# S4 convolution with a SwiGLU gate on one core: mirrored token tiles, 32x32 tiles in the tokens' second transform stage, and halved first and last steps

## The chip, the cores and the metric

The kernel runs on one core of one Trainium2 chip. The metric is device microseconds of one execution, as the median of several runs. TensorE is called PE below, its weight loads PEld; VectorE is DVE, ScalarE is ACT, GpSimd is POOL, and SyncE, which issues most DMAs, is SP.

## What is computed

`u` holds 2048 tokens of 512 channels. The tokens are normalised, and the result goes two ways: through a long convolution along time, whose kernel of 2048 taps is generated from 128 complex modes a channel, and through a feed-forward network with 1792 hidden channels. The output is the input plus the convolution times the gate. Cut to what matters (`A`, `Bc`, `Cc` and `dt` come from the other inputs):

```python
xn = _layernorm(u)
P = exp((dt * A)[:, :, None] * l)                       # 512 x 128 x 2048
K = einsum("dn,dnl,dn->dl", Cc, P, dt * Bc).real
y = irfft(rfft(pad(xn^T)) * rfft(pad(K)))[:, :2048]     # length 4096, per channel
s = y^T + xn * Dskip
h = (silu(xn @ w_gate) * (xn @ w_up)) @ w_down
out = u + s * silu(h)
```

## The kernel before, in words

**Stages.** The convolution is done by transforms as matmuls. Time t is written as 32 * t1 + t2, with 64 values of t1 and 32 of t2. A token tile `j` of 16 holds 128 rows: two values of t2 by the 64 values of t1; before, they are the neighbours t2 = 2j and 2j + 1. Stage 1 of the tokens (L549) transforms over t1 with fp16 halves, six matmuls of 512 columns a tile; ACT copies both results (L553), and they go to DRAM as `ax_d` (L554). The taps of the convolution are generated channel by channel (POOL L1061 and L1069, ACT L1084 to L1086, DVE L1104 and L1110, PE L1136), transformed over t1 (L1169) and written to `ak_d`.

Stage 2 goes over eight groups `n` of frequencies by two halves `c` of the channels, 16 blocks in all. Each block loads 512 KB of `ak_d` and 512 KB of `ax_d` into the buffers `ak` and `ax`, and the matrices `gj` of its group once. A block of the taps (L1222, called a k block below) and a block of the tokens (L1229, an x block) have each 16 fp32 matmuls of 256 columns, on tiles of the PE array of 64 rows by 32 columns, eight side by side, so in two rounds. A matmul in fp32 shows as two records in the trace. ACT copies the taps' result out of PSUM (L1239); DVE multiplies it with the tokens' in four instructions (L1247, L1249) and POOL combines these (L1251, L1252). After two blocks an inverse over frequencies follows (L1269, 32 matmuls on tiles of 32 by 32, 16 side by side, so also two rounds), whose result ACT and DVE take out (L1277, L1279) and SP writes to `bs_d` (L1281). After the eighth group of a channel half, the final step can begin (L1316): SP loads `bs_d` (L450, 512 KB), the input again (L1301) and the gate, four matmuls give the convolution of two token tiles and a channel half, DVE multiplies by the gate (L1335), POOL adds the input (L1338) and SP and ACT issue the output (L1342). The last two token tiles, 14 and 15, are done one by one over all channels (L1316, L1323, L1324, L1326).

The network runs beside this in units: 24 matmuls of 256 columns give a gate or an up projection of 256 tokens by 256 hidden channels (L685), ACT and DVE apply silu and the product (L706, L708) and split it into fp16 halves (L710 and L711), and six matmuls of 512 columns a token tile add it to the down projection (L727). L736 is the silu of its result. The weights are loaded in 512 KB pieces, their sum of squares taken on ACT (L590), a power of two as scale made of it on DVE (L621 to L625), and they are split into a high fp16 half on ACT (L655) and a low one on DVE (L656).

**Start.** SP loads the token tiles, `idh` (an identity for transposes) and the weights. DVE takes mean and variance (L485, L486) and an inverse root by three steps of Newton for two tiles at once (L491 to L499, eleven instructions), ACT and DVE make the fp16 halves (L511 to L513), PE transposes them (L522) and DVE copies them out (L528).

**Order.** A planner simulates tasks with given durations. The order of the tasks is a string, `LIST`, two characters a task; the places of the buffers in one SBUF arena are another, `PLACES`. The planner then only assigns eight PSUM banks and fills gaps of PE before the first units with warm-up matmuls (L1425). Each engine works through its own part in order. A DMA waits in its issuing queue until the eighth one before it in that queue has landed.

Of the kernel before, what the change touches and what calls it, by code (L numbers as in the profile page):

```python
# [9 lines left out]
F32 = mybir.dt.float32  # L10
# [9 lines left out]
P = 128  # L20
# [17 lines left out]
SWITCH = 0.095  # L38
TRANSPOSED, TR_US = 4, 1.7
# [11 lines left out]
    "(h(k%B(m$f(d$c$d)1%4$g)2$k$l$n%6%A%C(l(n(w&L&M(x%D)U$h$i$j)3%E)$$o)]$m$t%<%=%>)^%G&U&V&W(q(o(p(J(K)F):%F$u%H%I$p"
    "%?$q$r%L%M&i)G)%)&&`$s%@&a%J&X);)<$v(r%K-<&c&d&e&N)=)>&j%N%O(i)'&f&O).)/)0(^-=)?&P-A-B-C(j&Q&R->&Y&l&g&o&p&]&^(N"
    "(O(P(Q-?(y(z&m&n&S&T(s(t&Z&[)_-@-D-M({-F)H(u(v)`(|-Q)g-K)h-H-Z-E-J-R-O-G)I)P-L-N-U-X-I)Q#I)R-Y#F-[(}-S-T)i-n-w)j"
    "-]-a-e-j-b-W-P-V-^-l)@-o-g.+.,.--p-q-s)S-h-i-k.*)4)T-c-d)A)#-u-v-x)B-r)()C)D-_-t.../-f.0)5)*-m-y-z)))+),.1)E-`-{"
    "-|.8.9.3.4.2.;)V)W.:.>.6.<.5.7.G.B%P)X)Y.E.F.?.@.D.M.[.A.C.H)a)-)c.I.Z.N)b)6)7)d-}.&.=.J#H)8)9.%.$.#.'.).r.b.c%W"
    "%X)J%i%j.O%k)L.P)k)l)s)t.v.()K)M.w.x)Z.K.R)[.L*%.d.e.T.U*&*'.W)N)O)u._*.*/.V.].X.f.Q.s.t.u.S&b.Y.a.^.`%n.g)e)f%R"
    ")v)}.y.h.i%l.j.m&k.k%Q%V%`%o%p)m%m)o%q.l)n)p*#*$*6/,*7.n.o)q%T*:*<.{.|%U.q%a%d/'.p%e*8*9.z.}%S*;*=%r&)%f%b%c)r*("
    "**/$/#/%/)/&/()w)y/+/2/3///1/5&'/4/6/-/.)x/0/*/:/</A/7*>)z){*?*0*2/G*)*+)|/8/9/B*@%Y*A*1/>/;/@*,*-%Z/=/?/D/N*3%]"
    "/H/`%[%^%s%_/a*H*[/P/R*c/I%t/b%u/_/c/C/E/K&s/O/J/L%v/M&w/Q*B*D/d*4*5/F*C*E%w/S*F&x*I*J*L&v&t&u&z/e/t*K&q&{/T&r&|"
    "&y'#&}','-%x*d*G'$/U/g*M*N/V'%/Y'./W'/'>'?/f/Z'&*k*l*s0K'5'6*O*t*u*v/X/[''/]'0'@'B/j'3'C/m'E'F/o/n/^'1*P%y*Q*X'D"  # L60
    "*Y%z&#'7'2%{*e'*'+/h/i%g&$&%&&'(/s04*f/q%h/p*]/z&(%|%}&**^0(*Z/w0'/u050L/k'4/v/l*_*`*R*T/y/{/}/|/r0#/x0$*S00*U0="
    "'90?06070P0Q0R*V*W*g*a*b0M0N*}0O090S+#0+0-08':*w';'<020;0T0U0V'K+$0)0*0:0,*h0.')0<0/0103*x0W0>0@'='80%0&0e0X0s0Y"
    "0[0^0_0a+%0`0A0B*m*n0b0Z0]*o*p0d*i*j0C0G'J0t*y0F+&0D'I*q0E+*'A0h'P'^0H0m*r++1&0f*z*{*|0k0l+'0g0i+(+)+,1%1<+.0J0I"
    "0|0n0j0c+-1=1>1?0o0p0z+=+D+E1@1#0u+/0{0v0}0q0r1A1,+L1-0x+M#G1/1'0w0y1('G+0+1+21)1++31B1C1.101L1E1F'H'O'T+:'L'M1*"
    "1G1a'Q1J'N'R+;'g1D1$1112+<'S1K131H'p'q1Q1N+4'r+5'h'i1P'U+T141518+U't'_16'`+V'V171T191;'w+W1m1I+6+71R1S1U1M'u1n1V"
    "1W+>1X1:1t+X1Y1['v'x1v+?1`1Z1x2*1u1w+Y+@+A1O1]'X2)+8+9'j's1^'[']'k'l1_'m'Y'b+Z'n+[1q'c2+2,'Z'd1o1i1k'e'f1s2-2.2/"
    "+F+H'W+]1p1r1g1h1j+G+I1d1f+N1b1c1e20+J+K21+P22231l'a1y+^2=252429+B+C+O+Q'o2F2726282:1z+_+`1{+a2D2E2;2>2Y2[2]2?2@"
    "2G+b+g2Z2L+R2A2H2U2B+c2<2M2r2C2I2N+S2c+h+i2_2e3k5-2O2Q2W+d2q2u2P2R2S2T+o2V2s+k2t3^2^2`2a2b2d2J2K2v2w+j+l+e+f1|2$"
    "2#3m3`1}2%2&2x+m+n2X2f2g3n3o3a2h3l3_3q3p3t2y3d4S3u3s2(+p3r3w3c3b3g3h3v3f2'2i2k+y2|2j5+4_,%2l2m3e2n3#3$3%3',&,'3&"
    "2o3(2z2{2}+w,(3i2p3j3x4'4(3)3*3.,-,.3y3z3+4{4$3931,53|334%3}494)32354&3,3-,)7K30344#3=3{+q3/+x3B3:3D3F3;3<3@,*3A"  # L70
    "3C4Q4*36374a+s3>3?3H,++r,,+t3G3I3K3M3N483O3P3J3Q+u3L,6,7+z+{+|+},#38+v3E3R3S3T,$70474:4<4;4=4?5,4A5l4T4V4R4>4@4C"
    "3U4,3Y3X3V4U,8,93W3Z4B4W4b4d4-4/4[4X4.7J5.505/4Y4Z4^4]4+40437/4`4e424144463]3[454c4g4f4h4i4j4k4z,/,0,17f,2,34y51"
    "557g5452534D4K4E,:575Q5R5w4F4G4H564N4O4P4|4}4I4J,45$4L,>,?5#5(5'4l4m5%5&4M4v5k6Z4s,;4n4o5)4w4x4p4q,F5*,@,A4r585x"
    "4t4u,<,=595B,G,H5C5D5?5@5<5=,I5S5T5y5:5;5A5V5m5U5W5X5>5Z5Y,B5{,C5z5|6%5o6$6#5[5]5}6[6'8(5n6]656_5p5q,X5s6&5F,J5r"
    "665t,K6`6^6a6b,D,E,L,M5u67686h,`,a6A5v6(6,,h6c,i,p6)6d6f626-6*6e6:6/6960636=6;6<6>6?5E5G5I5H5J5M5N6@,N,O,V6g6i81"
    "6j5K6.6k6+645L5P6l6n6m6o6B6F6p,W6C7.6D615O6q6r6E6J7^7L6G6H,q7[,r,P7@5^,Q6I6K,R5b775c6L7R5e5h5i6s6z5f,S7I,b6{5d,Y"
    "6t6w6x7%6y6}7#,c7$6u6v5_5`715a6M6N7M7N7O,Z7;7)7]7C7(6W7B6X6Y6Q6R6O6P897273747&6S7*7:7D5g7E7A6T6U7_7a6V6|7F76,[7'"
    "78,],^,d,e,_7x,s,t7`7<5j8A7y8B,j887Q,l7P877S79,T,U,y7+,k,m8I7w8.,u,v,z,{,f,g8/8@7=-&7e,n,},o-'8J8%7p7z8:8<7b7c7U"
# [1394 lines left out]
```

## Time and profile before

| | |
|---|---|
| median of three runs | 581.22 us (581.16 to 582.86) |
| the profiled execution | 585.73 us, of which its span in the trace 583.8 us |
| granted clock of PE, mean | 0.997 |
| busy: PE, PEld | 570.9 us (98%), 409.1 us (70%) |
| busy: DVE, ACT, POOL | 422.5 us (72%), 342.6 us (59%), 325.8 us (56%) |
| moved by DMA | 93.62 MB; from HBM 56.40 MB read, 32.90 MB written |

A row of the slices gives the busy share of an engine in tenths for 40 equal slices of the span, 14.6 us each. A row of the groups gives engine, operation, output and input, the number of records, then busy time and mean ns of one, then idle time before. A row of the timeline or of the chain gives the start in us, the length in us, the engine and the line; `x24` at its end counts the records in it, and a bracket gives the idle time before and what ended it. "ACTq" and "SPq" are the queues' own time of issuing DMAs.

### The profile page before, as it was taken

The page shows a single profiled execution, that of the slowest core. Times are in us where ns is not written, and L with a number is a line of the kernel's source. Part 1 is how long each engine was busy: PE and PEld are TensorE (multiplying, and loading weights), DVE is VectorE, ACT ScalarE, POOL GpSimd, SP SyncE. Part 2 cuts the span into 40 slices and gives each one's busy share as a digit, 9 for nine tenths or more (in the row PEclk, how much of TensorE's full clock was granted, in tenths as well). Part 3 has the DMA queues.
Part 4 walks back from the last instruction along what each step waited for, and adds up shares of the span by engine and source line. Part 5 has one row for each costly group of instructions (what it writes and reads, how often), then busy time and mean ns, then how long its engine had stood idle before and what let it go on. Part 6 is the DMA issues. An engine that isn't in the chain of part 4 may idle for free.

```text
span 583.8 us, 18173 instructions
## 1 busy us (share of the span) xinstructions
PE 570.9 (98%) x7523; PEld 409.1 (70%) x7523; DVE 422.5 (72%) x980; ACT 342.6 (59%) x699; POOL 325.8 (56%) x301
## 2 busy tenths in 40 slices
PE   8999999999999999999999999999999999999976
PEld 3788885476885687848776688766866665678732
DVE  6878889537689787985889969877768585653342
ACT  5997677658565367777867889847652423321011
POOL 0154522479986369649799699879135155312140
PEclk9999999999999999999999999999999999999989
DMA  7886542341006150256622086378798878889986
GB/s 245 241 292 199 165 154 72 56 172 43 10 4 125 38 137 2 73 121 206 120 57 69 25 218 123 116 196 231 253 226 246 283 231 258 220 263 260 248 239 176
DMA packets 112434, 93.62 MB, mean 160 GB/s; under 512 B 51104, under 2 KB 96928, under 8 KB 112352
## 3 DMA queue, kind: packets, MB, share of 16 engines
q1 hardware_dynamic: 109856, 90.10, 55.4%
q10 hardware_dynamic: 2496, 2.36, 1.4%
q8 instruction: 59, 0.97, 0.7%
q14 instruction: 23, 0.19, 0.1%
HBM read 56.40 MB, written 32.90 MB: 153 GB/s over the span
## 4 chain that ended last, share of the span: by engine, by line
PE 93%; DMA 3%; ACT 1%; issue 1%; SPq 1%; DVE 0%; ACTq 0%; DVEq 0%
PE p L685 50%; PE p L727 25%; PE p L1136 5%; PE p L1222 3%; PE p L1229 3%; PE p L1316 2%; PE p L1269 2%; DMA arena<-bs_d 2%; PE p L549 2%; PE p L1169 2%; DMA wd<-in_B_w_gate_dram 1%; SPq L471 1%; PE p L785 1%; ACT wg L590 0%; ACTq L1342 0%
## 5 line engine op out<-in xcount | busy, mean ns | idle before, releaser
L685 PE MATMUL p<-arena,wg 128*128 128x256 f16 x1344 | 154.6, 273 | 0.5 <-ACT arena L553 0.5
L685 PE MATMUL p<-arena,wu 128*128 128x256 f16 x1344 | 154.9, 273 | 0.0
L727 PE MATMUL p<-wd,arena 128*128 128x512 f16 x672 | 152.5, 380 | 0.0
L685 PEld LDWEIGHTS <-wg 128*128 128x128 f16 x1344 | 130.2, 98 | 21.6 <-issue 2.8
L685 PEld LDWEIGHTS <-wu 128*128 128x128 f16 x1344 | 130.4, 98 | 20.3 <-issue 2.9
L727 PEld LDWEIGHTS <-arena 128*128 128x128 f16 x672 | 64.0, 98 | 76.0 <-issue 6.1
L1069 POOL TENSOR_TENSOR arena<-arena 128x1536 f32<-128x1536 f32 x32 | 90.8, 2842 | 24.5 <-PE p L1136 7.5
L708 DVE SCALAR_TENSOR_TENSOR p<-p,shc,arena 128x512 f32<-128x512 f32 x56 | 42.1, 755 | 49.7 <-PE p L685 35.1
L1061 POOL TENSOR_TENSOR arena<-arena 128x1024 int32<-128x1024 int32 x32 | 62.4, 1955 | 15.6 <-DVE arena L821 5.4
L710 ACT CAST arena<-p 128x512 f16<-128x512 f32 x56 | 32.4, 587 | 65.8 <-DVE p L708 38.7
L706 ACT ACTIVATE arena<-p,inv 128x512 f32<-128x512 f32 x56 | 38.6, 689 | 54.7 <-PE p L685 43.0
L711 DVE TENSOR_TENSOR arena<-p,arena 128x512 f16<-128x512 f32 x56 | 37.9, 683 | 19.2 <-ACT arena L710 16.1
L1104 DVE TENSOR_TENSOR arena<-arena,p 128x512 f32<-128x512 f32 x64 | 43.6, 681 | 7.2 <-ACT p L1085 4.4
L1338 POOL TENSOR_TENSOR arena<-arena 128x512 f32<-128x512 f32 x12 | 15.1, 1267 | 56.5 <-DVE arena L1335 22.9
L1085 ACT ACTIVATE p<-p,halfpi 128x512 f32<-128x512 f32 x64 | 41.8, 660 | 1.4
L1086 ACT ACTIVATE p<-arena 128x512 f32<-128x512 int32 x64 | 37.6, 602 | 7.5 <-PE p L1169 3.7
L1084 ACT ACTIVATE p<-arena 128x512 f32<-128x512 int32 x64 | 38.5, 605 | 5.3 <-DVE arena L711 3.1
L1251 POOL TENSOR_TENSOR arena<-arena 128x512 f32<-128x512 f32 x16 | 20.3, 1274 | 28.6 <-DVE arena L1247 13.6
L1252 POOL TENSOR_TENSOR arena<-arena 128x512 f32<-128x512 f32 x16 | 20.4, 1275 | 26.0 <-PE p L1169 13.1
L1136 PEld LDWEIGHTS p<-arena 128*32 128x32 f32 x2048 | 29.4, 110 | 4.8 <-issue 2.7
L1110 DVE SCALAR_TENSOR_TENSOR arena<-arena,p 128x256 f32<-128x256 f32 x64 | 26.4, 413 | 8.6 <-ACT p L1086 5.1
L1136 PE MATMUL p<-arena 128*32 128x64 f32 x2048 | 32.2, 220 | 0.0
(182 smaller groups left out, 792.4 us busy)
## 6 DMA issues: line engine op xcount, KB each, us to landing
ax_d<-arena SPq DMA_DIRECT2D x32, 256.0 KB, 3.0
ak_d<-arena SPq DMA_DIRECT2D x16, 512.0 KB, 5.9
arena<-ak_d SPq DMA_DIRECT2D x16, 512.0 KB, 4.6
arena<-ax_d SPq DMA_DIRECT2D x16, 512.0 KB, 5.2
bs_d<-arena SPq DMA_DIRECT2D x32, 256.0 KB, 4.1
arena<-in_A_u_dram SPq DMA_DIRECT2D x62, 128.0 KB, 3.7
arena<-in_B_w_down_dram SPq DMA_DIRECT2D x14, 512.0 KB, 5.3
arena<-bs_d SPq DMA_DIRECT2D x14, 512.0 KB, 8.2
```

The lines of the kernel that those rows point to most:

```text
L685: T.matmul(pg.t[:, i * 256:(i + 1) * 256].rearrange("p (a t) -> p a t", a=2), w[:, wl, d, i * P:(i + 1) * P], x[:, :, xl, d, :], start=(k ...
L706: add("ACT", 0.69, lambda: S.activation(sg.f32(), pg.t, AF.Silu, scale=inv[:, c, 0:1]), rd=[pg], wr=[sg], c=1, pr=e)
L708: add("DVE", 0.75, lambda: V.scalar_tensor_tensor(pu.t, pu.t, shc[:, c:c + 1], sg.f32(), op0=ALU.mult, op1=ALU.mult), rd=[sg], wr=[pu], c= ...
L711: add("DVE", 0.7, lambda: V.tensor_tensor(hh.view(F16)[:, 512:1024], pu.t, hh.view(F16)[:, 0:512], op=ALU.subtract), rd=[pu], wr=[hh], c=1 ...
L727: T.matmul(z.t, h[:, hl, i * 256 + t * P:i * 256 + (t + 1) * P], w[:, wl, i], start=(c == 0 and i == 0 and k == 0), stop=(c == NC - 1 and ...
L1061: G.tensor_tensor(a, h_[:, :, :, None].to_broadcast([P, 2 * GT, 4, 8]), l_[:, :, None, :].to_broadcast([P, 2 * GT, 4, 8]), op=ALU.add)
L1069: G.tensor_tensor(e, p_[:, :, :, None].to_broadcast([P, 3 * GT, 4, 8]), q_[:, :, None, :].to_broadcast([P, 3 * GT, 4, 8]), op=ALU.mult)
L1084: add("ACT", 0.62, lambda: S.activation(tc_.t, a(), AF.Abs, scale=SIN_SCALE), rd=[an], wr=[tc_], pr=pr)
L1085: add("ACT", 0.7, lambda: S.activation(tc_.t, tc_.t, AF.Sin, bias=halfpi, scale=-1.0), rd=[key("ones")], wr=[tc_], c=4, pr=pr)
L1086: add("ACT", 0.62, lambda: S.activation(ts.t, a(), AF.Sin, scale=SIN_SCALE), rd=[an], wr=[ts], pr=pr + 0.2)
L1104: V.tensor_tensor(o[:, :, 0:64].rearrange("p d (s j) -> p d s j", s=2), e[:, :, 0:64].rearrange("p d (s j) -> p d s j", s=2), t[:, :, None ...
L1136: T.matmul(kt[h * 32:(h + 1) * 32, (r * GD + dd) // 4], o[:, ri, dd + h, 64:96], o[:, ri, dd + h, 0:64], start=(ri == 0), stop=(ri == 1), ...
```

## The change

Token tile `j` now holds t2 = 16 + j and its mirror 16 - j (tile 0: 16 and 0), so that stage 2 of the tokens can work on sums and differences of the two. In stage 1 ACT copies one of the two results and DVE makes the sum and the difference (two new instructions for each of 15 tiles; ACT has one copy less there, tile 0 keeps both). The sums and differences are stored in `ax_d` as separate groups, 32 rows each. An x block has still 16 fp32 matmuls, now on tiles of 32 by 32, so in one round; its results lie in four PSUM banks, 256 columns each, instead of two full ones. k blocks and inverses are as they were. `gj` shrinks from 320 to 256 KB a group, `bs_d` gets an order of rows in which every final step reads contiguous pieces of 4 KB.

In the first steps, the first gate weight is loaded ahead of token tiles 2 and 3, in the place of `idh`, which moves to ACT's queue; an ACT table is loaded early; tiles 0 and 1 are normalised one by one, with two steps of Newton (7 instructions for one tile, 9 for two); the first gate weight is split in halves, so that the first gate unit, in four parts, can begin on a half. In the last steps, the down projection of the last token tile is done in two column halves (84 matmuls of 256 columns for 42 of 512), its silu likewise, and the final step of tiles 14 and 15 per channel half. The planner's constants differ a little, and `LIST` and `PLACES` are new throughout. Lines move: L685 is now L717, L727 is L760 (its halves L769), L1222 and L1229 are L1267 and L1275, L1269 is L1320, L1316 is L1365 (halves L1372), L553 is L573 and L575, with the new DVE lines L577 and L578.

Three places in the new order. The first is PE in stage 2, before: `p_` are PSUM banks, `wg` the gate weights, L1222 is a k block, L1229 are two x blocks in a row, and L685 a gate unit.

```order
L1222 MATMUL p_105<-arena 32x256
L1222 MATMUL p_106<-arena 32x256
L1229 MATMUL p_99<-arena 32x256
L1229 MATMUL p_102<-arena 32x256
...
L1229 MATMUL p_101<-arena 32x256
L1229 MATMUL p_103<-arena 32x256
L685 LDWEIGHTS wg
L685 MATMUL p_104<-arena,wg 128x256
```

PE in stage 2 of the changed kernel, at an x block (L1275) between a gate unit (L717) and an inverse (L1320):

```order
L717 LDWEIGHTS wg
L717 MATMUL p_101<-arena,wg 128x256
L1275 MATMUL p_99<-arena 32x256
L1275 MATMUL p_103<-arena 32x256
...
L1275 MATMUL p_100<-arena 32x256
L1275 MATMUL p_104<-arena 32x256
L1320 MATMUL p_102<-arena 32x256 x4
L1320 MATMUL p_105<-arena 32x256 x4
```

The x block's 16 matmuls go to four banks instead of two, and it stands between a unit of the network and an inverse, where the two of before stood behind a k block. Counted over all of PE's order, changes between one shape of tiles and another are 101 before and 128 now.

The second place is DVE at the start, before: L513 makes the low halves of the tokens, L621 to L625 the scale of the first gate weight (`scw`), L528 copies transposed tokens, L600 is a cast for the weights' norms, and L656 the low half of the first gate weight.

```order
L513 SCALAR_TENSOR_TENSOR arena<-arena,rstd 128x512
L621 TENSOR_SCALAR ssq<-p_99 128x1
L610 TENSOR_SCALAR scw<-ssq 128x1
...
L528 COPY arena<-p_101 128x512
L513 SCALAR_TENSOR_TENSOR arena<-arena,rstd 128x512
L528 COPY arena<-p_100 128x512
L600 CAST hsq<-ssq 128x2
...
L656 SCALAR_TENSOR_TENSOR wg<-wd,scw,wg 128x1024
```

The same place of DVE in the changed kernel, where L532 is L513, L646 to L650 are L621 to L625, L547 is L528 and L680 is L656:

```order
L532 SCALAR_TENSOR_TENSOR arena<-arena,rstd 128x512
L646 TENSOR_SCALAR ssq<-p_101 128x1
L635 TENSOR_SCALAR scw<-ssq 128x1
...
L532 SCALAR_TENSOR_TENSOR arena<-arena,rstd 128x512 x2
L625 CAST hsq<-ssq 128x1
L547 COPY arena<-p_100 128x512
L547 COPY arena<-p_104 128x512
L547 COPY arena<-p_102 128x512
L547 COPY arena<-p_99 128x512
L680 SCALAR_TENSOR_TENSOR wg<-wd,scw,wg 128x4x128 x2
```

The four copies of transposed tokens now stand together, and the low half of the weight, in two parts, right behind them.

The third place is ACT near the end, before: L706 and L710 are the silu and the cast of a hidden unit, L1342 issues outputs.

```order
L1342 DMA out_dram<-arena 64x2x256
L706 ACTIVATE arena<-p_104,inv 128x512
L1342 DMA out_dram<-arena 64x2x256 x3
L710 CAST arena<-p_102 128x512
L1342 DMA out_dram<-arena 64x2x256
L706 ACTIVATE arena<-p_103,inv 128x512
L1342 DMA out_dram<-arena 64x2x256
L710 CAST arena<-p_101 128x512
L710 CAST arena<-p_100 128x512
L1342 DMA out_dram<-arena 64x2x256 x3
```

ACT near the end of the changed kernel, where L739 is L706, L743 is L710, L1400 is L1342 and L781 is the silu of the down projection:

```order
L743 CAST arena<-p_104 128x512
L743 CAST arena<-p_101 128x512
L1400 DMA out_dram<-arena 64x2x256
L739 ACTIVATE arena<-p_104,inv 128x512
L743 CAST arena<-p_105 128x512
L1400 DMA out_dram<-arena 64x2x256 x5
L781 ACTIVATE arena<-p_100,zsc 128x256
```

One issue of an output stands ahead of the last hidden units' silu and cast, where there were six. The diff, cut to its core:

```diff
 SWITCH = 0.095
+BN = 2 * P + 6
...
+    "###&#%#)#'#(#*#L#P#M#Q#S#N#+#l#O#K#W#X#$#J#`#g#I#Z#A#n#o#H#_#b#a#,#m#R#p#Y#/#h#|#i#q#U#c#[#B&0#]&2#.#^&5#V#T#t#v"
...
-                x = dma_free + 1.9
+                x = dma_free + 1.75
...
-    return max(size / 255e3, pieces * 1.3e-3)
+    return max(size / 265e3, pieces * 1.3e-3)
...
+    def rows(v, h, j0, nj=1):
+        if h == 0:
+            return v[:, 16 + j0:16 + j0 + nj]
+        t2 = 16 - j0 if j0 else 0
+        if nj == 1:
+            return v[:, t2:t2 + 1]
+        return v[:, 0:16:15] if j0 == 0 else v[:, 16 - j0:14 - j0:-1]
...
-    ax_d = dram.tile([64, 2, 32, D], F32, name="ax_d")
+    ax_d = dram.tile([64, 2, 2, 16, D], F32, name="ax_d")
...
-    bs_d = dram.tile([2, 4, 4, 2, P, HD], F32, name="bs_d")
+    bs_d = dram.tile([2, 16, BN, HD], F32, name="bs_d")
...
-            V.tensor_scalar(v, mv[:, js, 1], 1e-5, 0.5, op0=ALU.add, op1=ALU.mult)
+            V.tensor_scalar(v, mv[:, js, 1], 1e-5, 1.0 / 4.5, op0=ALU.add, op1=ALU.mult)
             V.tensor_scalar(y.bitcast(I32), v.bitcast(I32), -0.5, 1593268703.0, op0=ALU.mult, op1=ALU.add)
-            for _ in range(3):
...
+            square()
+            V.scalar_tensor_tensor(y, r, 1.5, y, op0=ALU.subtract, op1=ALU.mult)
+            square()
+            V.scalar_tensor_tensor(r, r, 5.0 / 3.0, r, op0=ALU.subtract, op1=ALU.mult)
+            V.scalar_tensor_tensor(y, r, 1.25, y, op0=ALU.add, op1=ALU.mult)
...
+        xs, xd = xas
+        to = ax_d[:, :, 0, j], ax_d[:, ::-1, 1, j]
+        add("ACT", 0.6, lambda: S.copy(xd.f32(), pa[1].t), rd=[pa[1]], wr=[xd], c=5 if j < 4 else 2, pr=pr)
+        if j == 0:
+            add("ACT", 0.6, lambda: S.copy(xs.f32(), pa[0].t), rd=[pa[0]], wr=[xs], c=5 if j < 4 else 2, pr=pr)
+        else:
+            add("DVE", 0.7, lambda: V.tensor_tensor(xs.f32(), pa[0].t, xd.f32(), op=ALU.add), rd=[pa[0], xd], wr=[xs], c=5 if j < 4 else 2, pr=pr)
+            add("DVE", 0.7, lambda: V.tensor_tensor(xd.f32(), pa[0].t, xd.f32(), op=ALU.subtract), rd=[pa[0]], wr=[xd], c=5 if j < 4 else 2, pr=pr)
-            xa = xas[h]
-            add("ACT", 0.6, lambda h=h, xa=xa: S.copy(xa.f32(), pa[h].t), rd=[pa[h]], up=[xa], c=5 if j < 4 else 2, pr=pr)
...
+        if nm == "g" and c == 0:
+            half = lambda a, i: a.rearrange("p (k f) -> p k f", k=ND)[:, :, i * P:(i + 1) * P]
+            for i in range(2):
+                add("ACT", 0.6, lambda i=i: S.activation(half(hi, i), half(b.f32(), i), AF.Copy, scale=sc), rd=[b, key("sg0")], up=[k, key(f"wh0{i}")], c=1)
+            for i in range(2):
+                add("DVE", 0.68, lambda i=i: V.scalar_tensor_tensor(half(lo, i), half(b.f32(), i), sc, half(hi, i), op0=ALU.mult, op1=ALU.subtract),
+                    rd=[b, key(f"wh0{i}")], up=[k, key(f"wl0{i}")], c=1, port=True)
...
-            add("PE", 1.75, lambda: (mm((2,), (0,)), mm((0, 1, 2), (1,))), rd=[xT[b], key(f"w{nm}{c}")], wr=[pg], up=up, pr=pr)
+            add("PE", 0.44, lambda: mm((2,), (0,)), rd=[key("wl00" if nm == "g" else "wu0")], wr=[pg], up=up, pr=pr)
+            add("PE", 1.31, lambda: mm((0, 1, 2), (1,)), rd=[xT[b], key(f"w{nm}{c}")], wr=[pg], up=up, pr=pr)
...
+        if b == NB - 1 and t == 1:
+            for q in range(2):
+                def part(q=q, z=z[q]):
+                    h = hh.view(F16).rearrange("p (l n) -> p l n", l=2)
+                    w = wt["d"][:, c].rearrange("p l (i d) -> p l i d", i=2)
+                    for i in range(2):
+                        for k, (hl, wl) in enumerate(((0, 0), (0, 1), (1, 0))):
+                            T.matmul(z.t[:, 0:HD], h[:, hl, i * 256 + t * P:i * 256 + (t + 1) * P], w[:, wl, i, q * HD:(q + 1) * HD],
+                                     start=(c == 0 and i == 0 and k == 0), stop=(c == NC - 1 and i == 1 and k == 2))
+                add("PE", 0.66, part, rd=[hh, key(f"wd{c}")], wr=[z[q]], up=[key(f"down{idx}")], pr=ffn_due(pos) + W["dn"])
...
-            g = gjs[n] = buf(f"gj{n}0", 2560, "gj")
-            load(lambda: g.f32(), gj[n], [g], 327680, 128, pr)
+            g = gjs[n] = buf(f"gj{n}0", 2048, "gj")
+            load(lambda: g.f32(), gj[n], [g], 262144, 128, pr)
...
-            g = gjs[n].f32()[:, 0:256].rearrange("p (q m) -> p q m", q=4)
+            g = gjs[n].f32()[:, 0:128].rearrange("p (q m) -> p q m", q=4)
             for ri in range(2):
                 for q in range(4):
                     for p in range(2):
-                        T.matmul(pt[p].t[q * 32:(q + 1) * 32, ri * 256:(ri + 1) * 256],
-                                 g[p * 64:(p + 1) * 64, q, ri * 32:(ri + 1) * 32], a[p * 64:(p + 1) * 64, q],
-                                 start=True, stop=True, tile_position=(p * 64, q * 32))
-        add("PE", 0.9, mm, rd=[b, gjs[n]], wr=pt, up=dst, c=2, pr=s2_due(n, c), f32=4)
+                        r = slice((2 * p + ri) * 32, (2 * p + ri) * 32 + 32)
+                        T.matmul(pt[2 * p + ri].t[q * 32:(q + 1) * 32, 0:256], g[r, q], a[r, q],
+                                 start=True, stop=True, tile_position=(r.start, q * 32))
+        add("PE", 0.9 if nm == "k" else 0.47, mm, rd=[b, gjs[n]], wr=pt, up=dst, c=2, pr=s2_due(n, c), f32=4 if nm == "k" else 7)
         return pt
...
-            add("SP", 0.52, lambda q=q, b=b: sy.dma_start(bs_d[c, m, q].rearrange("k p d -> p k d"), b.f32().rearrange("p (k d) -> p k d", k=2)),
-                rd=[b], up=[key(f"bs{c}")], c=0, dma=dma_us(262144, 256))
+            add("SP", 0.52, lambda q=q, b=b: sy.dma_start(bs_rows(c, 4 * m + q, 0, ((2, P), (3, 2))), b.f32().rearrange("p (k d) -> p k d", k=2)),
+                rd=[b], up=[key(f"bs{c}")], c=0, dma=0.9)
...
-        src = bs_d.rearrange("c m q k (g s) d -> c k (m q) g s d", s=16)[:, k, :, :, s0:s0 + 2 * nj]
         chs = range(cs.start // HD, cs.stop // HD)
         for h in chs:
-            load(lambda h=h: bt.f32().rearrange("p (c x) -> p c x", c=len(chs))[:, h - chs[0]], src[h].rearrange("n g s d -> n g (s d)"), [bt],
-                 524288 // len(chs), 128, pr, rd=ready)
+            for first, lo, n in ((0, 0, 1), (33, 1, 1), (2, 2, 2)) if j0 == 0 else ((2 * j0, 0, 2 * nj),):
+                load(lambda h=h, lo=lo, n=n: bt.f32().rearrange("p (c s d) -> p c s d", c=len(chs), d=HD)[:, h - chs[0], lo:lo + n], bs_rows(h, 0, first, ((BN, 16), (32, 8), (1, n))),
+                     [bt, key(f"bt{tag}{h}")], 131072 * n, 128, pr, rd=ready)
...
+        if nj == 1:
+            for q in range(2):
+                def part(q=q):
+                    b = bt.f32().rearrange("p (c s d) -> p c s d", c=2, d=HD)
+                    for h in range(2):
+                        T.matmul(py.t[h * 64:(h + 1) * 64, q * HD:(q + 1) * HD], j2_t[:, h * 64:(h + 1) * 64], b[:, q, h], start=True, stop=True,
+                                 tile_position=(0, h * 64))
+                add("PE", 0.53, part, rd=[key(f"bt{tag}{q}"), key("j2")], up=[bt, py, key(f"py{tag}{q}")], c=2, pr=pr, f32=6)
...
-    load(lambda: idh_t, idh, [key("idh")], 32768, 128, -28.0)
-    for j in (2, 3):
-        x_load(j)
+    add("ACT", 0.6, lambda: nc.scalar.dma_start(idh_t, idh), up=[key("idh")], pr=-28.0, dma=0.13, root=True)
+    add("ACT", 1.4, lambda: S.activation(zsc[:, 2:3], halfpi, AF.Identity), rd=[key("ones")])
...
-    ln_group(0, 2)
+    for j in (2, 3):
+        x_load(j)
+    ln_group(0, 1)
+    ln_group(1, 1)
```

More of the change, by code (lines that the diff above doesn't have):

```diff
@@ L51 @@
[L51 to L55, printed above, removed]
@@ L718, in down @@
         if c == 0:
-            zps[b, t] = bank(f"z{b}{t}", "p")
+            zps[b, t] = [bank(f"z{b}{t}{q}", "p") for q in range(2)] if b == NB - 1 and t == 1 else bank(f"z{b}{t}", "p")
         z = zps[b, t]
@@ L1341, in final @@
         for h in range(2):
[L1342 removed]
+            add(("SP", "ACT")[h], 0.62, lambda h=h: (sy, nc.scalar)[h].dma_start(rows(ov, h, j0, nj)[:, :, cs], vw(ot)[h * 64:(h + 1) * 64]), rd=[ot], up=[key("out")], c=0,
                 dma=dma_us(131072, 64 * nj), pr=e)
```

181 lines of the change are left out of this document (98 added, 83 removed).

## The prediction

> **What bounds the kernel now.** I read the page first: span, busy times, slices and shares of the chain.
>
> ```profile
> span 583.8 us, 18173 instructions
> PE 570.9 (98%) x7523; PEld 409.1 (70%) x7523; DVE 422.5 (72%) x980; ACT 342.6 (59%) x699; POOL 325.8 (56%) x301
> ...
> PE   8999999999999999999999999999999999999976
> ...
> PEclk9999999999999999999999999999999999999989
> DMA  7886542341006150256622086378798878889986
> ...
> PE 93%; DMA 3%; ACT 1%; issue 1%; SPq 1%; DVE 0%; ACTq 0%; DVEq 0%
> ```
>
> PE is busy in 570.9 of 583.8 us at a full clock and is 93% of the chain, so time is PE's time plus its few gaps: in the first slice, and in the last two. But DMA stands at eight tenths or more in most slices from the 25th on, which is why the gaps at the end need a look of their own. Next come the chain and the timeline of PE; they give the price of a block, by its neighbours:
>
> ```profile
> 20.11 2.62 PE p L685 x24
> ...
> 412.58 2.73 PE p L685 x24
> ...
> 457.89 1.42 PE p L1269 x60
> ...
> 486.47 1.02 PE p L1229 x32
> 487.50 0.86 PE p L1222 x32
> 488.36 0.86 PE p L1229 x32
> ```
>
> A gate unit costs 2.62 us behind another and 2.73 behind a block of another shape. A k or x block costs 0.86 behind one of its shape and 1.02 otherwise. So a change of shape costs 0.16 into a block and 0.11 back. The gaps at the end, in the timelines of PE and ACT, and the last inverse and the last load of `bs_d` in the chain:
>
> ```profile
> 558.57 1.08 PE L1316 MATMUL p<-arena,j_t 128*64 128x256 f32 x8
> 562.81 4.50 PE L1316 MATMUL p<-arena,j_t 128*64 128x512 f32 x20 [3.16 <-DVE arena L711]
> 567.24 10.53 PE L727 MATMUL p<-wd,arena 128*128 128x512 f16 x48
> 577.70 1.08 PE L1316 MATMUL p<-arena,j_t 128*64 128x512 f32 x4
> ```
> ```profile
> 557.15 4.25 ACTq L1342 DMA_DIRECT2D out_dram<-arena  x3
> 561.45 0.58 ACT L710 CAST arena<-p 128x512 f16<-128x512 f32 x1 [7.30 <-issue]
> ```
> ```profile
> 513.23 1.42 PE p L1269 x60
> 514.66 5.33 PE p L1316 x48
> ...
> 546.23 3.48 PE p L1316 x31
> 549.71 10.34 DMA arena<-bs_d
> ```
>
> From 558.57 to 567.24 PE does 28 records of the final step. At 5.33 us for 48 these are 3.1, and the stretch lasts 8.67: some 5 us are lost (I use 5.1, with the change of shape). Two things lose them. The cast L710 stood behind three issues of outputs on ACT's queue, and the last load of `bs_d` was issued only at 549.71, when final steps had freed its buffer, and landed at 560.05.
>
> **The change, part by part.** The profiled execution took 585.73 us, its span and 1.9 around it. The median is 4.5 lower; I take differences from the profile to the median unchanged.
>
> *The x block.* It goes from two rounds of eight tiles to one of sixteen. The inverse is the only work that shows sixteen tiles of 32 by 32, in two rounds; one of its first rounds, and the groups:
>
> ```profile
> 457.82 0.71 PE L1269 MATMUL p<-arena 32*32 32x256 f32 x32
> ```
> ```profile
> L1222 PE MATMUL p<-arena 64*32 64x256 f32 x512 | 17.4, 379 | 0.6 <-issue 0.6
> L1229 PE MATMUL p<-arena 64*32 64x256 f32 x512 | 17.2, 378 | 0.0
> ...
> L1269 PE MATMUL p<-arena 32*32 32x256 f32 x512 | 12.3, 386 | 1.2 <-issue 1.2
> ```
>
> Here 32 records, a new x block's count, take 0.71 as the modelled end has it, about 0.64 to the next round's start, the change of 0.16 included: 0.48 without it. Bounds: half an old block, 0.43, and half the inverse's 1.42 less half a change, 0.63. I take 0.48, since it is the same work. Sixteen blocks save 16 x (0.86 - 0.48) = 6.1 us (3.7 to 6.9).
>
> *Shapes.* The order has 27 more changes of shape. Seventeen lead into k and x blocks (0.16), ten back (0.11): 3.8 us lost, or 3.2 by the starts of the next instructions. The rows thus say that a change costs 0.1 to 0.16. The Trainium skill (TensorEngine Tiling (Array Packing), section Key Properties) says that a change of tiling mode drains TensorE, and so speaks against a change that makes more of them; without such a drain the sum would be 3.8 us lower. The 0.86 and 1.02 of the same line agree with the page.
>
> PE's other items: 42 down matmuls of 512 columns become 84 of 256. 48 took 10.53, 0.219 each; a unit's 24 of 256 columns take 2.62, 0.109 each, so 84 cost 9.17 for 9.21: nothing, though a term of +0.2 for the changes between banks. Net for PE: -6.1 + 3.8 + 0.2 = -2.1 (-3.7 to +0.3).
>
> *First steps.* Rows at the start:
>
> ```profile
> 5.82 4.52 DMA wd<-in_B_w_gate_dram
> ```
> ```profile
> 2.25 0.59 SPq L450 DMA_DIRECT2D idh_t<-in_idh_dram  x1
> ```
> ```profile
> 18.63 1.03 PE L685 MATMUL p<-arena,wg 128*128 128x256 f16 x8 [0.51 <-ACT arena L553]
> ```
> ```profile
> 6.07 0.17 DVE L491 TENSOR_SCALAR va<-mv 128x2 f32<-128x2 f32 x1
> ...
> 8.04 0.16 DVE L499 SCALAR_TENSOR_TENSOR rstd<-rt,rstd 128x2 f32<-128x2 f32 x1
> ...
> 16.74 0.42 DVE L528 COPY arena<-p 128x512 f16<-128x512 f16 x1
> ...
> 18.15 1.28 DVE L656 SCALAR_TENSOR_TENSOR wg<-wd,scw,wg 128x1024 f16<-128x1024 f32 x1 [0.42 <-ACT wg L655]
> ```
> ```profile
> 16.98 1.13 ACT L655 ACTIVATE wg<-wd,scw 128x1024 f16<-128x1024 f32 x1
> ```
>
> The first gate unit begins at 18.63, last released by a copy of stage 1; its weight landed at 10.34 and was split at 16.98 to 18.11 on ACT and from 18.15 on DVE. Issued third, in the place of `idh` at 2.25, the weight lands at about 6.8 if its transfer still takes 4.52. `idh` on ACT's queue is needed by the first transpose only. The eleven steps of Newton take 2.13, so 0.2 each; 7 + 7 + 9 in place of 11 + 11 are one more, no matter. By the new order on DVE, statistics and Newton of tiles 0 to 3, two scales and the low halves come first, then the four copies of L528 at 0.42. I put these one behind the other by the rows' lengths: the copies end at about 16.7 and the weight's high half at 16.0. The unit begins at about 17.1, so -1.5. Against it, some ten small instructions of 0.2, of which PE would wait out about four, come ahead of the next weight's low half on DVE: +0.8. Taken: -0.7 (-1.5 to 0).
>
> *Tokens' sums on DVE.* Rows for its price:
>
> ```profile
> 388.28 0.69 DVE L1247 TENSOR_TENSOR arena<-p,arena 128x512 f32<-128x512 f32 x1 [2.28 <-PE p L1229]
> ```
> ```profile
> L553 ACT COPY arena<-p 128x512 f32<-128x512 f32 x32 | 18.1, 591 | 2.3 <-PE p L549 2.2
> ```
>
> Thirty instructions by 0.69 are 20.7 us more on DVE, fifteen by 0.59 are 8.9 less on ACT. DVE is idle in 161 of 583.8 us and nothing reads `ax_d` before the first x block, at about 388, so I cost it at nothing. The sums wait for PE and for ACT's copy; queued behind them on DVE are the network's products, and PE waits for these when its banks run out. If DVE's idle time doesn't cover that, three such waits of 0.69 are +2 us. The writes of `ax_d` on SP are 32 as before; the final step's first load in three pieces adds four issues, and 64 KB less for each `gj` go the other way.
>
> *Tail.* After the last down matmul:
>
> ```profile
> 578.88 0.42 DVE L1323 TENSOR_TENSOR arena<-p,arena 128x256 f32<-128x256 f32 x1 [5.35 <-PE p L1316]
> ...
> 580.14 0.43 DVE L1324 TENSOR_TENSOR arena<-arena 128x256 f32<-128x256 f32 x1
> ```
>
> Now two rounds on PE and four DVE instructions follow, to 580.57, then the output lands and the span ends at 583.8. In halves, only the last channel half follows: one round (0.43, half of an old block) and one pair on DVE (0.81, from 578.88 to 579.69 by the starts at this spacing of 0.42) less. -1.2; bounds -1.6 and -0.5, if the silu of the half is late.
>
> *The end stall.* In the new order one output issue, not six, stands ahead of the last units on ACT: that loss goes. Late next is the load. The last inverse ends at 514.66 and the last `bs_d` lands at 560.05, 45.4 us on. In the new order, by the prices above, PE has 42 us of work between the last inverse and the last four final steps, so at the old pace PE would wait 3 us again; but buffers come free earlier (six final steps stand together 35 us before the end, where before a group stood at 546.23, 31 us before it). Where DMA is full, as in the windows of SP with share and GB/s last:
>
> ```profile
> 540.00:550.00 10.00, 1.00 1.05 245
> 550.00:560.00 10.00, 1.00 1.05 256
> ```
>
> an earlier issue buys less than it seems. I take half of 5.1: -2.5 (-5.1 to 0).
>
> *Sum.* -2.1 - 0.7 - 1.2 - 2.5 = -6.5: profiled 579.2, median 581.22 - 6.5 = 574.7.
>
> **Rivals.**
>
> *B. The DMA stream sets the end.* By the sizes in the two programs, SP moves as much behind the last `ak_d` write as before. For it: the share of 1.05 from 540 to 560. Against: PE waits only 5 us there. The last `ak_d` write comes 2.6 us earlier by PE's prices, so the time is 581.2 - 2.6 = 578.6.
>
> *C. The x block isn't shorter in effect.* Four products of 0.69 are 2.76 us of DVE a block, and an x block with a gate unit is 0.48 + 0.16 + 2.73 = 3.37 of PE. With the network's own DVE instruction of 0.68 to 0.75 a unit that is 3.5 on DVE, so every x block waits 0.15; 0.63 a block, the upper bound, gives the same. 16 x 0.15 = 2.4 less gained: 577.1. Against: before, the x blocks stand in pairs, and PE shows only 0.6 us idle at L1222 and none at L1229. The Trainium skill (the same page, section PSUM Bottleneck) holds that tiling speeds up TensorE but not the evacuation of PSUM, which is this rival.
>
> *D. Slower: the last loads come late.* The new order puts more final steps between the last inverse and the end, and they run in PE's order, so each us of a late load delays all down matmuls behind it. My forecast has 2.6 us of this wait. With 9.1, a last load 6.5 later than forecast, the gain is gone; another load's 10.34 on top gives 581.22 + 3.9 = 585.1. For it: the full DMA, the chain's row of 10.34. Against: equal bytes and earlier buffers.
>
> *E. All of it.* The whole 5.1 and the whole 1.5 of the start come in: 574.7 - 2.6 - 0.8 = 571.3.
>
> **How the numbers follow.** Forecast 0.48 (its own range 572.5 to 577), B 0.20, C 0.10, E 0.08, D 0.14. A measurement of this kernel tells 0.3%, 1.7 us, from no change. Faster than 579.5: all of the forecast, C and E, and 0.12 of B, 0.78. Within: the rest of B and 0.01 of D, 0.09. Slower: 0.13 of D. The range leaves out D's upper part and E's lowest: 570.5 to 581.5.
>
> **What would show it.** Right: x groups of 32 records at 0.45 to 0.65 us, no old one at 0.86; more blocks at 1.02 and units at 2.73; PE busy lower by 2 us; the first gate matmul near 17.1; behind the last down matmul 5 us, not 6.1; a gap of 1 to 4 us at the last final steps, ended by a load of `bs_d` rather than by L743. Wrong: gaps between x blocks ended by DVE's products (C); gaps spread over the stretch from the first k block on, each ended by a load (B); a gap of over 9 us at the end (D).

## The result and the profile after

The changed kernel takes 577.74 us (577.35 to 578.55, four runs), the kernel before 581.30 beside it: ratio 0.9934, 95% interval 0.9914 to 0.9955. A second comparison of both, unchanged, gave 577.5 against 581.36, ratio 0.9929 (0.9904 to 0.9954). So the change gains some 3.7 us, where -6.5 was forecast; the sign and the wide range (570.5 to 581.5) hold, but the time lies above the forecast's own range (572.5 to 577). One more execution of before, in the second comparison, took 980.19 us at a granted clock of 0.557; it is in none of the medians and ratios here.

The profiled execution of after took 578.55 us. Its page, with the rows that answer to those shown of before:

```profile
span 576.8 us, 18270 instructions
PE 565.2 (98%) x7570; PEld 405.9 (70%) x7570; DVE 440.9 (76%) x1006; ACT 334.7 (58%) x686; POOL 327.1 (57%) x301
PE   7999999999999999999999999999999999999996
PEclk9999999999999999999999999999999999999999
DMA  8888722251003171058005452697879987998997
PE 93%; DMA 2%; SPq 2%; DVE 1%; issue 1%; ACT 0%; DVEq 0%
```

PE is still nearly the whole time, and the dent of before in the last slice but one (a 7, with an 8 in the row PEclk) is gone. Against the first profile of before the span is 7.0 us shorter, twice what the medians say. That alone shows that one of the two executions isn't typical; the first experiment takes this up.

The chain of after has the new prices, with no new mechanism in them:

```profile
430.05 2.73 PE p L717 x24
432.78 0.64 PE p L1275 x32
433.42 2.73 PE p L717 x24
436.15 0.64 PE p L1275 x32
...
484.69 1.02 PE p L1267 x32
485.71 0.73 PE p L1275 x32
```

An x block (L1275) behind a gate unit takes 0.64 us, 0.48 and a change of 0.16, as read off the inverse's first round. Behind a k block, as in the last row, it takes 0.73. The units around it take 2.73 instead of 2.62. The groups show it for all 16 blocks, 12.3 us where before had 17.2, while k blocks (L1267) nearly keep their time, 16.5 for 17.4:

```profile
L1267 PE MATMUL p<-arena 64*32 64x256 f32 x512 | 16.5, 381 | 0.2 <-DVE arena L1293 0.2
...
L1275 PE MATMUL p<-arena 32*32 32x256 f32 x512 | 12.3, 386 | 0.8 <-issue 0.8
```

### The profile page after: what moved, and what is told of

Read it like the earlier page. It is cut to its first block, busy times and chain, and to the rows that moved or that the text cites. A ratio compares the mean times of both kernels' runs of the same rounds, so it can differ in the third digit from the quotient of the medians.

```text
span 576.8 us, 18270 instructions
## 1 busy us (share of the span) xinstructions
PE 565.2 (98%) x7570; PEld 405.9 (70%) x7570; DVE 440.9 (76%) x1006; ACT 334.7 (58%) x686; POOL 327.1 (57%) x301
## 4 chain that ended last, share of the span: by engine, by line
PE 93%; DMA 2%; SPq 2%; DVE 1%; issue 1%; ACT 0%; DVEq 0%
PE p L717 50%; PE p L760 24%; PE p L1181 5%; PE p L1267 3%; PE p L568 2%; PE p L1275 2%; PE p L1365 2%; PE p L1320 2%; PE p L769 2%; PE p L1214 2%; DMA arena<-bs_d 1%; DMA arena<-in_A_u_dram 1%; SPq L464 1%; PE p L830 1%; SPq L485 1%
## 5 line engine op out<-in xcount | busy, mean ns | idle before, releaser
L717 PE MATMUL p<-arena,wu 128*128 128x256 f16 x1344 | 154.6, 273 | 0.0
L717 PE MATMUL p<-arena,wg 128*128 128x256 f16 x1344 | 154.5, 273 | 0.0
L717 PEld LDWEIGHTS <-wg 128*128 128x128 f16 x1344 | 130.5, 98 | 21.4 <-issue 2.8
L717 PEld LDWEIGHTS <-wu 128*128 128x128 f16 x1344 | 130.2, 98 | 20.2 <-issue 3.7
L760 PE MATMUL p<-wd,arena 128*128 128x512 f16 x630 | 143.2, 379 | 0.0
L760 PEld LDWEIGHTS <-arena 128*128 128x128 f16 x630 | 59.7, 98 | 71.8 <-issue 6.1
L739 ACT ACTIVATE arena<-p,inv 128x512 f32<-128x512 f32 x56 | 37.7, 685 | 65.9 <-PE p L717 62.5
L743 ACT CAST arena<-p 128x512 f16<-128x512 f32 x56 | 32.6, 586 | 38.4 <-DVE p L741 31.9
L1293 DVE TENSOR_TENSOR arena<-p,arena 128x512 f32<-128x512 f32 x32 | 21.1, 685 | 13.9 <-PE p L1275 7.7
```

The source lines that it names most:

```text
L717: T.matmul(pg.t[:, i * 256:(i + 1) * 256].rearrange("p (a t) -> p a t", a=2), w[:, wl, d, i * P:(i + 1) * P], x[:, :, xl, d, :], start=(k ...
L739: add("ACT", 0.69, lambda: S.activation(sg.f32(), pg.t, AF.Silu, scale=inv[:, c, 0:1]), rd=[pg], wr=[sg], c=1, pr=e)
L760: T.matmul(z.t, h[:, hl, i * 256 + t * P:i * 256 + (t + 1) * P], w[:, wl, i], start=(c == 0 and i == 0 and k == 0), stop=(c == NC - 1 and ...
```

## The experiments

**Both kernels once more.** Nothing edited.

> The kernel before, unchanged, profiled a second time. My theory now: the 5 us lost around the last final steps (558.57 to 567.24 in the first profile) belong to that one execution, which took 585.73 us where the median is 581.3; a second profile then shows a span of about 579.5 us, and between the last inverse and the last down matmul some 60 to 61 us instead of 64.5 (59 of them work). Rival: the loss is in every execution, and the first profile was long for another reason; then that stretch is again 64 us or more. Time against itself: within 0.3% of 581.3 us by both.

> The changed kernel, unchanged, for a closer ratio and a second profile. If -3.6 us is right, 577.7 us and a ratio of 0.9938 within 0.001. The first profile has 58.1 us from the last inverse to the last down matmul, 128.7 from the first k block to the last inverse and 18.5 up to the first gate unit; all three should come again within 1 us if they belong to the kernel, and differ by more if they belong to the execution.

Before: 581.89 us against 581.36, ratio 1.002 (0.9996 to 1.0044). After: as above. The question is where the executions differ. I cut each at three points: the first gate unit, the first k block and the last inverse, up to the last down matmul. The windows of PE for both profiles of before (columns: stretch, its length, PE busy, granted clock, share of DMA, GB/s), first the one shown in the prediction, then the second:

```profile
18.60:384.40 365.80, 365.77 (x4570) 1.00 0.41 113
384.40:513.20 128.80, 126.66 (x2375) 1.00 0.84 240
513.20:577.80 64.60, 61.44 (x507) 0.97 0.92 252
```
```profile
18.70:384.50 365.80, 365.79 (x4576) 1.00 0.42 113
384.50:512.30 127.80, 126.03 (x2366) 1.00 0.84 242
512.30:573.90 61.60, 59.80 (x508) 1.00 0.95 257
```

And both profiles of after:

```profile
18.50:384.10 365.60, 365.60 (x4576) 1.00 0.41 112
384.10:512.90 128.80, 126.68 (x2404) 1.00 0.86 249
512.90:571.10 58.20, 57.82 (x532) 1.00 0.92 249
```
```profile
17.90:383.50 365.60, 365.60 (x4573) 1.00 0.40 112
383.50:510.50 127.00, 126.03 (x2393) 1.00 0.88 253
510.50:569.00 58.50, 57.68 (x533) 1.00 0.92 246
```

The first stretch is the same to 0.2 us in all four: there PE alone sets the time. The last one was 64.6 us in the first profile of before and 61.6 in the second. So 3 us of the loss that I had costed at 5.1 belonged to that execution: 61.6 where my theory said 60 to 61 and the rival 64 or more. After needs 58.2 and 58.5, with 57.7 to 57.8 busy: the end is now work.

Two things make these 3 us. PE's wait ahead of the 20 records of L1316 was 3.16 us in the first profile of before (the prediction shows the row) and is 1.80 in the second. And behind the longer wait the same 20 records took 4.50 us instead of 2.81, at a lower granted clock. The windows of PE over these records, first profile and second (the clock is the number behind the count):

```profile
562.81:567.24 4.43, 4.43 (x21) 0.61 0.94 278
```
```profile
560.65:563.39 2.74, 2.74 (x21) 1.00 0.94 284
```

So 1.4 us are wait and 1.7 are clock. The wait has the same cause in the second profile, three issues on ACT ahead of a cast (the timelines of ACT and PE):

```profile
554.87 4.38 ACTq L1342 DMA_DIRECT2D out_dram<-arena  x3
559.28 0.58 ACT L710 CAST arena<-p 128x512 f16<-128x512 f32 x1 [5.94 <-DMA out_dram<-arena]
```
```profile
560.65 2.81 PE L1316 MATMUL p<-arena,j_t 128*64 128x512 f32 x20 [1.80 <-DVE arena L711]
```

**The x block back in two rounds.** In `s2_mm` of after:

```diff
-                        r = slice((2 * p + ri) * 32, (2 * p + ri) * 32 + 32)
+                        r = slice(p * 64, p * 64 + 64)
...
-                                 start=True, stop=True, tile_position=(r.start, q * 32))
+                                 start=True, stop=True, tile_position=(p * 64, q * 32))
```

> The changed kernel with the matmuls of its x blocks back on tiles of 64 rows by 32 columns, so in two rounds of eight; order, banks and all else as they are. Each result then sums over 64 rows instead of 32, so the convolution is another one. If PE sets the pace and the round is what was gained, each of 16 blocks goes from 0.64 to 0.86 or 1.02 with the change of shape: by my price 16 x 0.38 less some four changes of shape that go, +5.4 us, so about 583.1. If DVE's products or loads set the pace of the blocks, the longer block is hidden: +0 to +2.5 us.

582.64 us, ratio to before 1.0012 (0.9991 to 1.0033): 5.1 us above after, where 5.4 was expected. An x block costs 0.86 behind a k block and 1.02 behind a unit again:

```profile
429.79 0.86 PE p L1275 x32
430.65 2.73 PE p L717 x24
433.38 1.02 PE p L1275 x32
```

All of it is PE's own work in the stretch from the first k block to the last inverse, 131.45 us where after has 126.03 and 126.68 (window of PE):

```profile
384.20:517.40 133.20, 131.45 (x2397) 1.00 0.82 241
```

The block's length counts in full, so PE sets the pace there and not DVE's products: with C's 2.4 us of waits only 3.0 would have been lost. The group of L1275 in after says the same, with 0.8 us of idle time before all 16 blocks. Rival C is out. Without the one round the time can't be told from that of before.

**The sums on DVE, three ways.** The sum made three times; then both results copied by ACT as before, with the difference on 16 of 512 columns; then only the difference cut to 16 columns:

```diff
-            add("DVE", 0.7, lambda: V.tensor_tensor(xs.f32(), pa[0].t, xd.f32(), op=ALU.add), rd=[pa[0], xd], wr=[xs], c=5 if j < 4 else 2, pr=pr)
+            def thrice():
+                for _ in range(3):
+                    V.tensor_tensor(xs.f32(), pa[0].t, xd.f32(), op=ALU.add)
+            add("DVE", 0.7, thrice, rd=[pa[0], xd], wr=[xs], c=5 if j < 4 else 2, pr=pr)
```
```diff
-            add("DVE", 0.7, lambda: V.tensor_tensor(xs.f32(), pa[0].t, xd.f32(), op=ALU.add), ...
-            add("DVE", 0.7, lambda: V.tensor_tensor(xd.f32(), pa[0].t, xd.f32(), op=ALU.subtract), ...
+            add("ACT", 0.6, lambda: S.copy(xs.f32(), pa[0].t), ...
+            add("DVE", 0.1, lambda: V.tensor_tensor(xd.f32()[:, 0:16], pa[0].t[:, 0:16], xd.f32()[:, 0:16], op=ALU.subtract), ...
```

> The changed kernel with the sum of every mirrored pair made three times over, which adds 30 instructions of 0.69 us, 20.5 us, to DVE in the first 340 us, as many as the change itself added; what is computed stays the same. If DVE's idle time hides the sums, as I costed them, the time stays within 1 us of the changed kernel's 577.7. If the network's units wait for DVE there, 2 us or more are added, and the change's own sums cost about that too.

> The changed kernel with stage 1 of the tokens taken out of PSUM as before the change: ACT copies both results, and DVE does the difference on 16 of 512 columns only, so sums and differences are not made and the convolution is another one. DVE has 19 us less to do, ACT 9 us more. If DVE's idle time hides the sums, as I costed them, the time stays at 577.5 within 1 us (the stretch from the first gate unit to the first k block at 365.6). If they cost something already, as their threefold cost of 13.8 us for 20.5 us more may mean, it is 574 us or less.

> The changed kernel with the difference of every mirrored pair made on 16 of 512 columns only, so the convolution is another one; DVE has 15 x 0.6 = 9 us less to do in the first 340 us, and no other engine has more. This is the clean form of the run before, which also gave ACT more to do. If the sums are hidden, as I costed them: the stretch from the first gate unit to the first k block stays at 365.6 us within 0.3, the time at 577.5 within 1. If they cost something: 2 us or more are gained there.

The clean form, less on DVE and nothing more elsewhere, took 577.24 us, ratio 0.9902 (0.9867 to 0.9936). Its first stretch, in the windows of PE:

```profile
18.50:384.10 365.60, 365.60 (x4576) 1.00 0.41 112
```

That is after's 365.6: the sums are hidden, as costed. But the cover ends there. Three times the sum took 591.34 us, 13.8 above after for 20.5 us of DVE. The timeline of PE at one place, and the chain of that kernel at the same place:

```profile
126.19 2.78 PE L720 MATMUL p<-arena,wu 128*128 128x256 f16 x24 [1.59 <-DVE arena L581]
131.62 4.45 PE L720 MATMUL p<-arena,wu 128*128 128x256 f16 x24 [2.64 <-DVE arena L581]
```
```profile
120.62 0.70 DVE arena L579
...
130.27 1.30 DVE arena L581 x2
```

Four tiles' sums stand together, 11 us of them instead of 5.5; a unit's matmuls on PE wait until the last of them has freed its bank, and the next unit's product stands behind them on DVE. In the whole kernel PE's waits for DVE at such units are 9.5 us. Behind two of the waits the 24 records of a unit took 4.45 and 4.46 us instead of 2.78, at a granted clock of 0.60 where the first row above has 1.00; that is 3.3 more of the 13.8.

With ACT in their place the time was 582.99, 5.5 above after; in its profile the stretch to the first k block grew to 369.9 us. Most of that lies at one place, as the timelines of ACT, DVE and PE show:

```profile
44.77 0.57 ACT L577 COPY arena<-p 128x512 f32<-128x512 f32 x1
```
```profile
45.37 0.17 DVE L578 TENSOR_TENSOR arena<-p,arena 128x16 f32<-128x16 f32 x1 [6.20 <-ACT arena L577]
45.46 1.28 DVE L688 SCALAR_TENSOR_TENSOR wg<-wd,scw,wg 128x1024 f16<-128x1024 f32 x1
```
```profile
43.59 3.62 PE L1487 MATMUL p<-ones 128*128 128x512 bf16 x16
```

ACT reached the copy late, DVE waited for it, and the low half of the next gate weight (L688) stood behind on DVE, at 45.46 where after has it at 40.95. PE could begin the next gate unit only behind it, at 47.04; the planner had put 16 of its warm-up matmuls there, 3.6 us. So that run prices this place in the order and not the sums, and its expectation was wrong on both sides.

**The start.** One run puts the statistics and Newton of tiles 2 and 3 behind the first gate unit (the first 85 tasks of `LIST` in another order); one loads the first gate weight behind the tokens again:

```diff
+for i in (75, 74, 72, 8):
+    LIST.remove(i)
+    LIST.insert(LIST.index(37) + 1, i)
```

> The changed kernel with the first 85 tasks in another order: the statistics and Newton of token tiles 2 and 3 come behind the first gate unit's work on DVE, ACT and PE, and the first weight's sum of squares behind the second tile on ACT. In the profile DVE waits 1.6 us for the loads of tiles 2 and 3, which now land at 9.6 to 11.4 behind the first weight, and what the first gate unit needs stands behind that wait. Theory: the first gate unit, at 18.5 in both kernels, comes at about 14, but DVE is busy nearly without a gap up to 24 us, so only its idle 1.6 us can be gained in all: about 576.3 us against 577.5. Rival: the queue order is the whole loss, and 3 us or more are gained, 574.5 or less. Second rival: the weights' loads bound the start, and nothing is gained.

> The changed kernel with the first gate weight loaded behind token tiles 2 and 3, as in the kernel before, and its sum of squares one place later on ACT. In the change the weight took 6.9 us to land instead of 4.5, and tiles 2 and 3 landed at 9.6 to 11.4 instead of 5.8 to 8.0; DVE waited 1.6 us for them. Theory: the two moves cancel; tokens land by 8, DVE doesn't wait, the weight lands at about 10.5 and its sum of squares is the later one; first gate unit at 17.5 to 18.5, time 577.0 to 577.5. Rival: the weight's early load is what the start is worth, and the first gate unit comes at 19.5 or later, 578.5 us. Second rival: the tokens' early load is worth 1.5 us or more, 576 us.

The rows of after behind this (DVE, ACT and SP at the start): the weight is issued at 2.25, but ACT gets it only at 9.18, so it took 6.9 us and not 4.5, and DVE waits for the tokens behind it.

```profile
10.41 0.69 DVE L499 BATCH_NORM_STATS2 st<-arena 128x6 f32<-128x512 f32 x1 [1.61 <-DMA arena<-in_A_u_dram]
```
```profile
9.18 1.06 ACT L615 ACTIVATE wg<-wd 128x1024 bf16<-128x1024 f32 x1 [1.86 <-DMA wd<-in_B_w_gate_dram]
```
```profile
2.25 0.59 SPq L464 DMA_DIRECT2D wd<-in_B_w_gate_dram  x1
```
```profile
18.53 2.79 PE L717 MATMUL p<-arena,wg 128*128 128x256 f16 x24
```

In the first run the gate unit began at 15.18 instead of 18.53, but the up unit at 26.82 instead of 22.48, and the time was 584.97 us. Part of this is a fault of my order (a small matmul for a later weight's norm stood ahead of the up unit and waited 1.66 us for DVE, behind the tokens; and 16 of the planner's warm-up matmuls, 3.63 us from 18.68 on, stood ahead of the tokens' transposes and are in the chain), so it doesn't price the start; it shows only that an early first unit alone gained nothing in this order. In the second run the first gate unit came at 18.62, as in after: the weight's and the tokens' early loads cancel, as its theory had it. Its time was yet 580.02 us (ratio 0.9953, 0.9931 to 0.9975), 2.3 above after; by the ratios to before it is 1.1 to 1.4, and the intervals overlap. In its profile the stretch from the first k block to the last inverse is 129.5 us where after has 127.0 and 128.8. Why that should come from a move at the start stays open.

**The tail.** Three output DMAs of earlier tiles, which after issues between the last steps, issued before them:

```diff
+for i, last in ((1950, 1941), (1840, 1950), (1877, 1974)):
+    LIST.remove(i)
+    LIST.insert(LIST.index(last) + 1, i)
```

> The changed kernel with three output DMAs of earlier tiles, which it issues at 570.3 to 571.6 between the last steps, issued before these. In its profile DVE ends 1.6 us behind the last down matmul where it was 2.9, but the last output lands 2.9 us after its issue where it was 2.2, and the first gain is given back. Theory: the last output shares the DMA engines with these three; issued earlier, they leave it alone, and the span from the last down matmul to the end goes from 5.7 to 6.2 us to about 5.0; 576.8 us. Rival: the landing time is that of the two halves' writes themselves, or the outputs only collide elsewhere; no change.

> The changed kernel with the weight behind the tokens, as in the run before, and the three outputs issued earlier at the end, as in the run on the tail. If both effects are what their profiles show (0 to 1.5 us at the start, 0.4 to 0.9 behind the last down matmul), 575.5 to 577 us; if either is only a shift of a wait, 577.5 us.

In after, DVE ends soon behind the last down matmul, as the chain and DVE's timeline have it:

```profile
561.91 9.17 PE p L769 x84
571.08 0.61 PE p L1372 x4
```
```profile
571.78 0.42 DVE L1381 TENSOR_TENSOR arena<-p,arena 128x256 f32<-128x256 f32 x1 [2.00 <-PE p L1372]
572.24 0.42 DVE L1382 TENSOR_TENSOR arena<-arena 128x256 f32<-128x256 f32 x1
```

From the last down matmul (571.08) to DVE's end (572.66) are 1.6 us, against 2.8 before (577.77 to 580.57): the forecast's 1.2. But the span ends 4.1 us later at 576.8, against 3.2 before. In the run with the three outputs moved, DVE ended at 572.17 and the span at 575.9, so 3.7, and the whole tail was 5.3 us, against 5.7 and 6.3 in after's two profiles and 6.0 and 6.1 in those of before. Its theory holds in the profile, but the times can't tell it: 577.76 us, ratio 0.9919 (0.9891 to 0.9946). With the weight's move added it was 579.11 (0.9950, 0.9928 to 0.9971), above both of its expectations, so that no version beats the changed kernel.

**The kernel before with its casts first.** Five outputs on ACT's queue moved behind the last casts:

```diff
+for i in [1864, 1918, 1828, 1837, 1891]:
+    LIST.remove(i)
+LIST[LIST.index(901) + 1:LIST.index(901) + 1] = [1864, 1918, 1828, 1837, 1891]
```

> The kernel before with five output DMAs of ACT's queue moved behind the last casts of the hidden units (L710), which they held up at the end. Two profiles of before lose 5.4 and 2.5 us between the last inverse and the last down matmul, both with a cast that ended late behind three such issues. Theory: the issues on ACT are this loss, so that the stretch goes from 61.6 to 60 us or less and the time to about 579.5 us. Rival: the last load of bs_d is as late (it landed at 557.9 in the second profile, where PE stood from 558.8 to 560.7), and at most 0.5 us are gained.

580.63 us, ratio to before 0.9991 (0.9972 to 1.001): not told apart by the times, and by the interval a gain of at most 1.6 us, where the theory asked for 1.9. In its profile PE has no gap at the place where it lost 1.8 us and more:

```profile
558.38 3.67 PE L1320 MATMUL p<-arena,j_t 128*64 128x256 f32 x28
561.98 10.53 PE L731 MATMUL p<-wd,arena 128*128 128x512 f16 x48
```

The stretch from the last inverse to the last down matmul is then 59.5 us, 2.0 less than in the second profile of before: in these profiles the issues on ACT were that loss, and the last load was not the later of the two. What the typical execution lost there is less sure, since the gain did not come in the times.

## Why the prediction was right in sign and too large

**The x block and the shapes** were right. 0.48 for the round, 0.16 and 0.11 for the changes and a net of -2.1 on PE agree with the rows and, from the other side, with the 5.1 us lost when the round is taken back. PE's busy time in the three stretches together fell by 2.3 us from the second profile of before to the second of after. PE's rows show no wait for a load at these blocks, though the chain of after's second profile goes through one load of `ax_d`, which landed at 500.63, 0.05 us before its block began.

**The end stall** was the mechanism named, six outputs on ACT ahead of the casts, but mis-sized. I took half of 5.1 us, which one execution showed; the other lost 2.0 by the same count (5.6 us for the 28 records that take 3.6 in the run with the casts first; the prediction's 3.1 for them was too little, its 5.1 was right). I had that execution's excess over the median, 4.5 us, in front of me and carried its differences over unchanged: this is the step that failed. I also called PE's clock full, though the row PEclk that I showed has an 8 there: 1.7 of the 5.1 were that clock. After still waits a little there, 0.4 and 0.8 us in its two profiles, for the load that I had put next in line:

```profile
553.38 1.95 PE L1365 MATMUL p<-arena,j_t 128*64 128x256 f32 x16 [0.38 <-DMA arena<-bs_d]
```

So by the profiles -1.2 to -1.6 was to be had, not -2.5.

**The tail** of -1.2 came on PE and DVE, and most or all of it was lost to the landing of the last output. That this shared the DMA engines with outputs that the new order leaves until then fits the run with the three outputs moved, but is not shown by its times. I had priced the instructions and taken the landing as it was.

**The first steps**, -0.7, gave 0.1 in the first pair of profiles and 0.8 in the second. The step that failed is the weight "at about 6.8 if its transfer still takes 4.52": it landed at about 9.2, and behind it the tokens became the late ones. The 0.8 that I set against the early unit doesn't show either (365.6 us in the stretch behind, for 365.8), so that the second pair's agreement with -0.7 is luck.

**The sums** at nothing: right, with the limit that the cover was far from enough for three times the sum.

Together: -2.1 on PE, -1.2 to -1.6 at the end, -0.1 to -0.8 at the start, about 0 for the tail, so -3.4 to -4.5, against -3.6 and -3.9 measured. The terms for the end, the start and the tail are read from single profiles; the times of the runs on them are too close to tell. Rival B's 578.6 and C's 577.1 lie nearer to the time than the forecast, but not for their reasons: PE hardly waits for loads, and the x blocks' pace is PE's. E's 571.3 needed the whole 5.1 and the whole 1.5. D asked for a wait of 9 us at the end; there was none over 1.

## What to carry to other kernels

Before a gap in a profile becomes a term of the sum, ask whether the profiled execution is as long as the median, and read the granted clock beside the gap: here 3 of the 4.5 us of excess were at that one gap, and half of them were matmuls at a lower clock. A transfer that is moved forward isn't moved alone: what it overtakes lands later, so price both. And an engine's idle share says little of its slack at one place: DVE stood at 76%, and 20 us more on it cost 14.

## What the runs showed of the hardware that was not expected

A 512 KB weight took 4.5 us to land when it was issued behind the tokens and 6.9 when it was issued ahead of four of their pieces. The first eight pieces of the tokens took 2.6 to 3.6 us to land in before and 3.3 to 6.9 in after: the place ahead in the queue didn't give the weight the engines alone.

A wait of PE can cost more than its length. In before's first profile and twice in the run with the sums thrice, PE stood for 3.16, 2.64 and 2.04 us, and the 20 or 24 records behind it took 1.7 us longer than elsewhere, at a granted clock of 0.60 or 0.61. Behind waits of 1.80, 1.59 and 1.34 us the clock stayed at 1.00. The length of the one wait doesn't decide it alone: in the run with the sums' copies on ACT the clock fell to 0.70 for 2 us behind a wait of 1.14.
